# Channel-attention plus channel-mix kernel: covariance rows of batch 1 moved into block 0's up projection, warm-up matmuls after the first x projection, squares in pairs, and a last block that computes its gates first

## Chip, cores, metric

One NeuronCore of one Trainium2 chip. The metric is device microseconds of one execution. All runs told of here count as fast ones. A run repeats only to a few microseconds (the kernel before took 530.3 to 534.9 us in the three calls below), so the text relies on ratios within one call (kernels that ran on the same chip, round by round) and, for where the time goes, on distances inside the profiles.

PE is TensorE, PEld its weight loads, DVE VectorE, ACT ScalarE, POOL GpSimd, SP the queue of SyncE.

## The reference, cut to what matters

Inputs q, k, v are (4, 6208, 256) in float32.

```python
qn = q / (norm(q, axis=1) + 1e-6);  kn = k / (norm(k, axis=1) + 1e-6)
a  = softmax(kn^T @ qn / tau)              # 256 x 256 for each of 4 batches
x  = v @ a                                 # 6208 x 256 for each batch
xk = mu_k * x + (1 - mu_k) * x_prev;  xr = mu_r * x + (1 - mu_r) * x_prev   # x_prev: the row before
out = sigmoid(xr @ w_r) * (relu(xk @ w_k) ** 2 @ w_v)                       # d_ff = 1024
```

A batch has 12 blocks of 512 rows and 64 rows over. The kernel runs 48 full blocks and one last block of 4 x 64 = 256 rows that gathers what is over ("left").

## The kernel before

Batch 0's covariance (k^T q and the sums of squares) comes first, alone. Then a loop over blocks, cut in eight steps j, interleaves on PE: the up projection of block i+1, the down projection of block i, the x projection (v times attention) of block i+2, and one *unit* (one row tile of the covariance of the next batch) in some of the steps. Per group of four units PE also adds up the squares (`group_norms`), and after batch 1's 49 units a chain of 16 small pieces makes its softmax.

```python
def unit_square(b, g, s):                      # ACT: squares of one row tile, 128 x 512
    rows, _ = rows_of(b, g)
    qk, qk2 = groups[b, g][:2]
    nc.scalar.activation(qk2[:rows, s], qk[:rows, s], AF.Square)

def up(i, fh):                                 # PE, then ACT
    ...
    nc.scalar.activation(kr[:, :m], kT_ps[:, :m], AF.Relu, scale=0.5 ** 0.5)

def down(i, j):                                # PE: a gate and 8 matmuls for each 128 rows
    ...
def finish(i, s):
    nc.scalar.activation(res[:, s], vr_ps[:, D:], AF.Tanh, scale=0.5)
    nc.vector.scalar_tensor_tensor(res[:, s], res[:, s], 1.0, vr_ps[:, :D], op0=OP.add, op1=OP.mult)
    if (s + 1) * P == size(i):
        if i < NBLK - 1:
            ...                                # one store of the block
        else:
            for b in range(B):                 # last block: four stores, one queue
                s, o = divmod(b * L, P)
                nc.sync.dma_start(out[b, NB * M:, :], res[o:o + L, s, :])
...
# order of the loads: w_k, group 0, v(1), group 1, w_r, w_v, v(2), group 2, then in the loop v(3), ...
halves()                                       # batch 0's softmax
x_first()                                      # x projection of block 0
v_transpose_pe(1, nc.scalar.copy)()            # needs v of block 1
early = units[:S + 1]                          # group 0 (1 row tile) and group 1 (4) of batch 1
for u in early:
    unit_matmul(*u, late=True)                 # needs k of group 1
for u in early[:3]:
    unit_square(*u)
keep_warm(4)                                   # matmuls that only keep PE busy
for i in range(-2, NBLK):
    for j in range(8):
        ...
        up(i + 1, j)
        ...
        if i == -1 and j == 6:
            v_transpose_pe(2, nc.vector.tensor_copy)()     # needs v of block 2
        if i == -1 and j == 7:
            group_norms(1, 0); group_norms(1, 1)
        slots = () if i < 0 else (1, 2, 3, 4, 5, 7) if i < 8 else (1, 3, 4, 5, 7)
        if j in slots and ...: unit()
```

Of the kernel before, what the change touches and what calls it, by code (L numbers as in the profile page):

```python
# [10 lines left out]
F32 = mybir.dt.float32  # L11
BF16 = mybir.dt.bfloat16
AX = mybir.AxisListType.X
AF = mybir.ActivationFunctionType
OP = mybir.AluOpType
# [3 lines left out]
def kernel(  # L19
# [13 lines left out]
    nc = tc.nc  # L33
    B, N, C = q.shape
# [48 lines left out]

    cov = {}
    groups = {}
    DIRECT = NB - 3

    def sizes(b):
        return [1] + [S] * (NB - 1) + ([S // 2] * 2 if b == 0 else [S])
# [5 lines left out]
    def rows_of(b, g):  # L95
        return (P if g else L), sizes(b)[g]
# [29 lines left out]
            nc.scalar.activation(qk2[:rows, :n, i, :], t_f[i][:rows, :n], AF.Square)  # L126

    def unit_square(b, g, s):
        rows, _ = rows_of(b, g)
        qk, qk2 = groups[b, g][:2]  # L130
        nc.scalar.activation(qk2[:rows, s], qk[:rows, s], AF.Square)

    def unit_matmul(b, g, s, late=False):
        rows, n = rows_of(b, g)
        t0 = g == order(b)[0] and s == 0
        te = g == len(sizes(b)) - 1 and s == n - 1
        if t0:

            cov[b] = (ps.tile([P, 2, C], F32, name="s_ps", tag="s_ps" if b else "vr_ps", bufs=1 if b else 2),
                      ps.tile([P, 2 * C], F32, name="ssq_ps", tag="ssq_ps" if b else "vr_ps", bufs=1 if b else 2))  # L140
        s_ps = cov[b][0] if b or g <= DIRECT else cov["s"]
        qk = groups[b, g][0]
        for ih in range(2):
            nc.tensor.matmul(s_ps[:, ih, :], qk[:rows, s, 1, ih * P:(ih + 1) * P],  # L144
                             qk[:rows, s, 0, :], start=t0 and ih == 0, stop=te,
                             skip_group_check=True)
        if s == n - 1 and not late:
            if b == 0 and g > DIRECT:
                norms_direct(g)
            else:  # L150
                group_norms(b, g)

    def group_norms(b, g):

        rows, n = rows_of(b, g)
        ssq_ps = cov[b][1]
        qk2 = groups[b, g][1]
        for u in range(n):
            nc.tensor.matmul(ssq_ps[32 * u:32 * (u + 1)], ones[:rows, :32],  # L159
                             qk2[:rows, u].rearrange("p i c -> p (i c)"),  # L160
                             start=g == (1 if u or b == 0 else 0), stop=g == (len(sizes(b)) - 1 if b else DIRECT), tile_position=(0, 32 * u),
                             skip_group_check=True)

    def norms_direct(g):

# [106 lines left out]
    def size(i):  # L272
        return M if i < NBLK - 1 else B * L
# [14 lines left out]
    def v_transpose_pe(i, evac):  # L288

        v_bf = st.pop((i, "v"))  # L290
        vT_ps = ps.tile([P, S, 2, P], BF16, name="vT_ps", tag="kT_ps", bufs=3)
        for s in range(S):
            for h in range(2):
                nc.tensor.transpose(vT_ps[:, s, h], v_bf[:, s, h * P:(h + 1) * P], ident)

        def go():
            vT = p2.tile([P, S, 2, P], BF16, name="vT", tag="vT", bufs=4)
            evac(vT, vT_ps)
            st[i, "vT"] = vT
        return go  # L300
# [18 lines left out]
    def x_first():  # L319

        xT = p2.tile([P, 2, M + 1], BF16, name="xT", tag="xT", bufs=3)
        st[0, "x"] = xT
        nc.vector.memset(xT[:, :, 0:1], 0.0)
        vT = st[0, "vT"]
        x_ps = [ps.tile([P, M], F32, name="xT_ps", tag="vr_ps", bufs=2) for dh in range(2)]
        for ih in range(2):
            for dh in range(2):
                nc.tensor.matmul(x_ps[dh], a_sb[:, 0, ih, dh * P:(dh + 1) * P], vT[:, :, ih, :],
                                 start=ih == 0, stop=ih == 1)
        nc.scalar.copy(xT[:, 0, 1:], x_ps[0])  # L330
        nc.vector.tensor_copy(xT[:, 1, 1:], x_ps[1])
# [66 lines left out]
    def down(i, j):  # L398

        s, h = divmod(j, 2)  # L400
        if s * P >= size(i):
            return
        kk = st[i, "kk"]
        if j == 0:
            st[i, "res"] = p2.tile([P, S, D], F32, name="res", tag="res", bufs=3)
        if h == 0:
            vr_ps = ps.tile([P, 2 * D], F32, name="vr_ps", tag="vr_ps", bufs=2)
            st[i, "vr"] = vr_ps
            xr = st[i, "xr"]
            for dh in range(2):  # L410
                nc.tensor.matmul(vr_ps[:, D:], xr[:, dh, s * P:(s + 1) * P], w_r_sb[:, dh, :],  # L411
                                 start=dh == 0, stop=dh == 1)
        vr_ps = st[i, "vr"]
        for fh in (range(3) if h == 0 else range(3, 8)):
            nc.tensor.matmul(vr_ps[:, :D], kk[:, fh, s * P:(s + 1) * P], w_v_sb[:, fh, :],  # L415
                             start=fh == 0, stop=fh == 7)

    def finish(i, s):
        if s * P >= size(i):
            return  # L420
        res = st[i, "res"]
        vr_ps = st[i, "vr"]

        nc.scalar.activation(res[:, s], vr_ps[:, D:], AF.Tanh, scale=0.5)  # L424
        nc.vector.scalar_tensor_tensor(res[:, s], res[:, s], 1.0, vr_ps[:, :D], op0=OP.add, op1=OP.mult)  # L425
        if (s + 1) * P == size(i):
            if i < NBLK - 1:
                b, t = blocks[i]
                nc.sync.dma_start(out[b, t * M:(t + 1) * M, :].rearrange("(s p) c -> p s c", p=P), res)
            else:  # L430
                for b in range(B):
                    s, o = divmod(b * L, P)
                    nc.sync.dma_start(out[b, NB * M:, :], res[o:o + L, s, :])



# [84 lines left out]
    keep_warm(7)  # L521
    halves()
    x_first()
    v_transpose_pe(1, nc.scalar.copy)()

    early = units[:S + 1]
    pos["mm"] = pos["sq"] = S + 1
    for u in early:
        unit_matmul(*u, late=True)
    for u in early[:3]:  # L530
        unit_square(*u)
    keep_warm(4)


    left_go = {}
    left = {}
    for i in range(-2, NBLK):
        for j in range(8):
            if j % 2 == 0:
                if j == 0 and i >= 1:  # L540
                    finish(i - 1, 3)
                elif j > 0 and i >= 0:
                    finish(i, j // 2 - 1)
            if j == 0 and 3 <= i + 5 < NBLK - 1:
                v_load(i + 5)
            if chain:
                piece = chain.pop(0)
                if piece is not None:
                    piece()
            if 0 <= i + 1 < NBLK:  # L550
                up(i + 1, j)
            if i >= 0:
                if j == 0 :
                    square(i, 7)
            if j > 0 and 0 <= i + 1 < NBLK:
                square(i + 1, j - 1)
            if i >= 0:
                down(i, j)
            if i + 2 < NBLK:
                n = i + 2  # L560
                full = 0 < n < NBLK - 1
                if j == 0 and full:
                    x_half(n, 0)
                if j == 2 and full:
                    x_half(n, 1)
                if j == 3:
                    mix_delta(n)
                if j in (4, 5):
                    mix(n, "xk", j - 4)
                if j == 7:  # L570
                    mix(n, "xr", 0)
            if j == 1 and 0 <= i + 1 < NBLK:
                mix(i + 1, "xr", 1)
            if i == -1 and j == 6:
                v_transpose_pe(2, nc.vector.tensor_copy)()
            if j == 5 and 3 <= i + 4 < NBLK - 1:
                v_transpose(i + 4)
            b = (i + 2) // NB
            if i == -1 and j in (3, 5):
                unit_square(*early[3 if j == 3 else 4])  # L580
            if i == -1 and j == 7:
                group_norms(1, 0)
                group_norms(1, 1)
            if i < 0:
                slots = ()
            elif i < 8:
                slots = (1, 2, 3, 4, 5, 7)
            else:
                slots = (1, 3, 4, 5, 7)
            if j in slots and pos["mm"] < len(units) and units[pos["mm"]][0] <= b + 1:  # L590
                unit()
            if i >= 0 and i % NB == 2 and j == 1 and i // NB < B:
                left_go[0] = left_x(i // NB)
            if i >= 0 and i % NB == 4 and j == 4 and i // NB < B:
                left_go[0][0]()
            if i >= 0 and i % NB == 6 and j == 4 and i // NB < B:
                left_go[0][1]()


# [33 lines left out]
```

## Time and profile before

534.54 us, median of 3 runs (534.12 to 535.59).

| what | value | view |
|---|---|---|
| profiled span | 532.8 us | page |
| PE, ACT busy | 95%, 82% | page |
| PE waiting, 60 to 526 us | 1.0 us in all | table of waits |
| first x projection, block 0's down stage | 41.82, 58.37 us | timeline |
| last block: first gate, last multiply's end, end of span | 525.19, 528.73, 532.8 us | timeline |

Lines of the page: the span, busy us of PE and ACT, and the clock granted to PE in 40 slices, in tenths.

```profile
span 532.8 us, 10152 instructions
...
PE 507.3 (95%) x3590; PEld 336.5 (63%) x3651; DVE 408.6 (77%) x962; ACT 434.4 (82%) x883; POOL 102.2 (19%) x143
...
PEclk9997999999999999999999999999999999999999
```

The table of waits of PE from 60 to 526 us (us in total, times, longest):

```profile
PE kT_ps L386 <- DVE xk L371: 1.0, 2, 0.5
```

The steady part has nothing to win for PE. The ends have. The clock, in windows of 3 us (length, then busy us of PE, PEld, DVE, ACT, POOL; then the granted clock, DMA share, GB/s):

```profile
42.00:45.00 3.00, 1.20 (x9) 0.40 (x8) 2.17 (x5) 0.59 (x1) 1.81 (x3) 1.00 1.42 195
45.00:48.00 3.00, 1.22 (x12) 0.70 (x9) 1.64 (x4) 2.06 (x3) 1.99 (x4) 0.59 1.46 198
48.00:51.00 3.00, 3.00 (x12) 1.51 (x10) 0.00 (x0) 0.63 (x2) 1.44 (x3) 0.50 1.46 195
51.00:54.00 3.00, 2.95 (x12) 1.16 (x11) 1.31 (x3) 1.93 (x4) 1.76 (x3) 0.77 1.45 197
```

The timeline of PE alone, around the start of block 0 (start, us, engine, line, operation, tiles, count, and in brackets the idle time before it and what ended it):

```profile
41.82 1.10 PE L328 MATMUL xT_ps<-vT,a_sb 128*128 128x512 bf16 x4 [0.29 <-DVE a_sb L256]
44.72 0.62 PE L294 MATMUL vT_ps<-ident,v_bf 128*128 128x128 bf16 x8 [1.80 <-DMA v_bf<-in_v_dram]
...
47.44 1.89 PE L144 MATMUL s_ps<-qk 128*128 128x256 bf16 x8 [1.78 <-DMA qk<-in_k_dram]
49.12 1.91 PE L444 MATMUL junk_ps<-fill,ones 128*128 128x512 bf16 x4
50.83 1.06 PE L386 MATMUL kT_ps<-xk,w_k_sb 128*128 128x512 bf16 x2
...
57.28 0.39 PE L159 MATMUL ssq_ps<-qk_464,ones 64*32 64x512 bf16 x1
...
57.93 0.60 PE L386 MATMUL kT_ps<-xk,w_k_sb 128*128 128x512 bf16 x2
58.37 0.38 PE L411 MATMUL vr_ps<-w_r_sb,xr 128*128 128x256 bf16 x2
```

Line 328 is block 0's x projection. PE then waits 1.80 us for v of block 1 and 1.78 us for k of group 1, and the clock falls to half: the eight covariance matmuls at 47.44 and the four warm-up matmuls at 49.12 take 0.43 us for each 512 columns and not 0.22. Line 386 is the up projection, line 411 a gate of the down stage.

The end, all engines:

```profile
525.19 0.38 PE L411 MATMUL vr_ps<-w_r_sb,xr 128*128 128x256 bf16 x2
...
525.40 1.36 PE L415 MATMUL vr_ps<-w_v_sb,kk 128*128 128x256 bf16 x8
...
526.48 0.10 PEld L415 LDWEIGHTS <-kk 128*128 128x128 bf16 x1 [0.43 <-DVE kk L396]
...
527.67 2.46 SPq L433 DMA_DIRECT2D out_dram<-res  x4
527.89 0.38 ACT L424 ACTIVATE res<-vr_ps 128x256 f32<-128x256 f32 x1 [0.71 <-PE vr_ps L415]
528.31 0.42 DVE L425 SCALAR_TENSOR_TENSOR res<-res,vr_ps 128x256 f32<-128x256 f32 x1 [0.67 <-ACT res L424]
```

The gate at 525.19 and its 8 matmuls, of which the eighth waits for a square until 526.48, then the second half; its tanh (527.89), its multiply (528.31), and four stores that one queue issues one after the other.

### The profile page before, as it was taken

Reading aid. Unit: us, or ns where it says so; the run is one execution under the profiler, and the core shown is the slowest. Engines: PE = TensorE matmul, PEld = TensorE weight load, DVE = VectorE, ACT = ScalarE, POOL = GpSimd, SP = SyncE. Lnnn points to the kernel's source line nnn. Section 1 sums busy time; section 2 is a strip of 40 time slices with the busy share of each in tenths; the row PEclk is TensorE's granted clock in tenths of the full one; section 3 lists DMA queues with packets and bytes.
Section 4 is the critical chain, followed back from the end, with each engine's and each line's share of the span. In section 5 each row is a group of like instructions: output and inputs, shape, how many; then the busy total and the mean of one; then the engine's idle time right before and its main releaser. Section 6 shows DMA issues by size and latency. Waiting matters only on the chain.

```text
span 532.8 us, 10152 instructions
## 1 busy us (share of the span) xinstructions
PE 507.3 (95%) x3590; PEld 336.5 (63%) x3651; DVE 408.6 (77%) x962; ACT 434.4 (82%) x883; POOL 102.2 (19%) x143
## 2 busy tenths in 40 slices
PE   4977999999999999999999999999999999999996
PEld 1453566666666666666666666666666666666675
DVE  4554787777898777777798777877898989888883
ACT  6884999898788888888778888888878777777773
POOL 0055423221311231322041322310030101000000
PEclk9997999999999999999999999999999999999999
DMA  8999999999599999999498999995286565433212
GB/s 302 421 283 185 190 191 199 197 168 132 76 208 157 166 196 156 157 168 163 84 189 152 133 198 175 137 189 115 61 138 139 103 139 112 110 86 94 80 41 98
DMA packets 143722, 83.76 MB, mean 157 GB/s; under 512 B 51700, under 2 KB 140088, under 8 KB 143672
## 3 DMA queue, kind: packets, MB, share of 16 engines
q0 software_dynamic: 65808, 33.01, 51.5%
q1 hardware_dynamic: 77856, 50.11, 37.9%
q8 instruction: 28, 0.46, 0.3%
q14 instruction: 22, 0.18, 0.1%
q10 hardware_dynamic: 8, 0.00, 0.0%
HBM read 78.71 MB, written 25.43 MB: 195 GB/s over the span
## 4 chain that ended last, share of the span: by engine, by line
PE 86%; DMA 7%; DVE 3%; ACT 1%; issue 1%; POOL 1%; SPq 0%; ACTq 0%
PE vr_ps L415 32%; PE kT_ps L386 29%; PE vr_ps L411 8%; PE xT_ps L315 7%; PE s_ps L144 6%; PE ssq_ps L159 2%; DMA f_339<-in_k_dram 2%; DMA f_235<-in_k_dram 2%; DMA qk<-in_k_dram 2%; DMA f_130<-in_k_dram 1%; DVE xk L371 1%; ACT kr L390 1%; DVE kk L396 1%; DVE res L425 0%; PE bank L194 0%
## 5 line engine op out<-in xcount | busy, mean ns | idle before, releaser
L390 ACT ACTIVATE kr<-kT_ps 128x512 bf16<-128x512 f32 (+1 forms) x392 | 232.9, 596 | 48.7 <-PE kT_ps L386 28.6
L415 PE MATMUL vr_ps<-w_v_sb,kk 128*128 128x256 bf16 x1552 | 233.1, 273 | 2.0
L386 PE MATMUL kT_ps<-xk,w_k_sb 128*128 128x512 bf16 (+1 forms) x726 | 219.9, 378 | 1.5 <-DVE xk L371 1.0
L415 PEld LDWEIGHTS <-kk 128*128 128x128 bf16 x1552 | 151.9, 98 | 58.7 <-DVE xT L308 0.6
L396 DVE TENSOR_TENSOR kk<-kr 128x512 bf16<-128x512 bf16 (+1 forms) x392 | 155.0, 415 | 7.7 <-ACT kr L390 7.1
L425 DVE SCALAR_TENSOR_TENSOR res<-res,vr_ps 128x256 f32<-128x256 f32 x194 | 81.2, 419 | 76.9 <-ACT res L424 74.9
L386 PEld LDWEIGHTS <-w_k_sb 128*128 128x128 bf16 x784 | 73.6, 98 | 36.8 <-issue 9.3
L144 PE MATMUL s_ps<-qk 128*128 128x256 bf16 (+1 forms) x392 | 73.2, 288 | 7.1 <-DVE qk L124 5.3
L317 ACT CAST xT<-xT_ps 128x512 bf16<-128x512 f32 x94 | 55.3, 588 | 29.3 <-PE xT_ps L315 29.1
L424 ACT ACTIVATE res<-vr_ps 128x256 f32<-128x256 f32 x194 | 74.0, 381 | 2.3 <-PE vr_ps L415 1.7
L411 PE MATMUL vr_ps<-w_r_sb,xr 128*128 128x256 bf16 x388 | 74.1, 273 | 0.7
L371 DVE SCALAR_TENSOR_TENSOR xk<-delta,mu_t,xT 128x512 bf16<-128x512 bf16 x96 | 71.4, 744 | 0.0
L371 DVE SCALAR_TENSOR_TENSOR xr<-delta,mu_t,xT 128x512 bf16<-128x512 bf16 x96 | 71.4, 744 | 0.0
L411 PEld LDWEIGHTS <-xr 128*128 128x128 bf16 x388 | 37.9, 98 | 46.0 <-issue 2.0
L118 POOL DMA_DIRECT2D qk<-in_q_dram x39 | 29.0, 742 | 181.4 <-ACT res L424 32.3
L315 PE MATMUL xT_ps<-vT,a_sb 128*128 128x512 bf16 x188 | 56.3, 381 | 0.0
L144 PEld LDWEIGHTS <-qk 128*128 128x128 bf16 (+1 forms) x392 | 38.7, 102 | 19.3 <-DVE qk L124 8.2
L278 POOL DMA_DIRECT2D v_bf<-in_v_dram x48 | 37.2, 776 | 66.6 <-DMA vT<-v_bf 62.2
L361 DVE TENSOR_TENSOR delta<-xT 128x1024 bf16<-128x1024 bf16 x48 | 33.2, 692 | 14.1 <-ACT xT L317 14.0
L118 POOL DMA_DIRECT2D qk<-in_k_dram x39 | 29.0, 743 | 2.6 <-DMA w_v_sb<-in_moe_w_v_dram 1.6
L315 PEld LDWEIGHTS <-a_sb 128*128 128x128 bf16 x188 | 18.5, 98 | 2.9 <-issue 0.6
L206 POOL TENSOR_TENSOR rn<-rn,half 128x4 f32<-128x4 f32 x3 | 3.2, 1073 | 63.1 <-DVE rn L203 63.1
(218 smaller groups left out, 242.8 us busy)
## 6 DMA issues: line engine op xcount, KB each, us to landing
out_dram<-res SPq DMA_DIRECT2D x48, 512.0 KB, 3.5
v_bf<-in_v_dram POOLq DMA_DIRECT2D x48, 256.0 KB, 7.9
qk<-in_q_dram POOLq DMA_DIRECT2D x36, 256.0 KB, 5.9
qk<-in_k_dram POOLq DMA_DIRECT2D x36, 256.0 KB, 8.0
vT<-v_bf SPq DMA_TRANSPOSE x45, 5.5
f_104<-in_q_dram SPq DMA_DIRECT2D x1, 512.0 KB, 3.8
f_106<-in_k_dram SPq DMA_DIRECT2D x1, 512.0 KB, 5.0
f_128<-in_q_dram SPq DMA_DIRECT2D x1, 512.0 KB, 5.8
```

The costliest lines, as they stand in the source:

```text
L118: nc.gpsimd.dma_start(qk[:rows, :n, i, :], qk_src(t, b, g))
L144: nc.tensor.matmul(s_ps[:, ih, :], qk[:rows, s, 1, ih * P:(ih + 1) * P], qk[:rows, s, 0, :], start=t0 and ih == 0, stop=te, skip_group_che ...
L315: nc.tensor.matmul(xT_ps, a_sb[:, b, ih, dh * P:(dh + 1) * P], vT[:, :, ih, :], start=ih == 0, stop=ih == 1)
L317: nc.scalar.copy(xT[:, dh, 1:], xT_ps)
L371: nc.vector.scalar_tensor_tensor(o[:, dh], st[i, "d"][:, dh], mu[:, dh:dh + 1], st[i, "x"][:, dh, :M], op0=OP.mult, op1=OP.add)
L386: nc.tensor.matmul(kT_ps[:, :m], w_k_sb[:, dh, fh * P:(fh + 1) * P], xk[:, dh, :m], start=dh == 0, stop=dh == 1)
L390: nc.scalar.activation(kr[:, :m], kT_ps[:, :m], AF.Relu, scale=0.5 ** 0.5)
L396: nc.vector.tensor_tensor(st[i, "kk"][:, fh, :m], kr[:, :m], kr[:, :m], op=OP.mult)
L411: nc.tensor.matmul(vr_ps[:, D:], xr[:, dh, s * P:(s + 1) * P], w_r_sb[:, dh, :], start=dh == 0, stop=dh == 1)
L415: nc.tensor.matmul(vr_ps[:, :D], kk[:, fh, s * P:(s + 1) * P], w_v_sb[:, fh, :], start=fh == 0, stop=fh == 7)
L424: nc.scalar.activation(res[:, s], vr_ps[:, D:], AF.Tanh, scale=0.5)
L425: nc.vector.scalar_tensor_tensor(res[:, s], res[:, s], 1.0, vr_ps[:, :D], op0=OP.add, op1=OP.mult)
```

## The change

Its intent: start block 0's up projection without waiting for covariance data, and put the first covariance rows of batch 1 into it where PE waits for ACT; keep PE busy with nine warm-up matmuls after the first x projection, so that the clock does not fall; spare ACT some fixed cost by squaring two row tiles at once; and shorten the last block's serial end.

```diff
     def unit_square(b, g, s):
-        nc.scalar.activation(qk2[:rows, s], qk[:rows, s], AF.Square)
+        if s % 2 == 0:
+            e = min(s + 2, n)
+            nc.scalar.activation(qk2[:rows, s:e], qk[:rows, s:e], AF.Square)
...
+    def last_block(i):
+        ...                                   # gates of both halves first
+        square(i, 7)
+        finish(i - 1, 3)
+        for s in range(SL):
+            nc.scalar.activation(res[:, s], r_ps[:, s], AF.Tanh, scale=0.5)
+        for s in range(SL):
+            for fh in range(8):
+                nc.tensor.matmul(y_ps[s], kk[:, fh, s * P:(s + 1) * P], w_v_sb[:, fh, :], ...)
+            nc.vector.scalar_tensor_tensor(res[:, s], res[:, s], 1.0, y_ps[s], op0=OP.add, op1=OP.mult)
+            for h in range(P // L):
+                (nc.sync, nc.scalar)[h % 2].dma_start(out[s * P // L + h, NB * M:, :], res[h * L:(h + 1) * L, s])
...
     x_first()
+    keep_warm(7)
     v_transpose_pe(1, nc.scalar.copy)()
+    keep_warm(2)
-    for u in early:
-        unit_matmul(*u, late=True)
-    for u in early[:3]:
-        unit_square(*u)
-    keep_warm(4)
...
-                if j == 7:
+                if j == 7 and n != 1:
                     mix(n, "xr", 0)
+            if i == 0 and j == 6:
+                mix(1, "xr", 0)
...
-            if i == -1 and j in (3, 5):
-                unit_square(*early[3 if j == 3 else 4])
+            if i == -1 and j in (5, 6):
+                for u in early[:2] if j == 5 else early[2:]:
+                    unit_matmul(*u, late=True)
+            if (i, j) in ((0, 1), (0, 5), (1, 3)):
+                unit_square(*early[{(0, 1): 0, (0, 5): 1, (1, 3): 3}[i, j]])
-            if i == -1 and j == 7:
+            if i == 0 and j == 7:
                 group_norms(1, 0)
+            if i == 2 and j == 0:
                 group_norms(1, 1)
+            elif i == 0:
+                slots = (3, 5, 7)
+            elif i == 1:
+                slots = (1, 2, 4, 5, 7)
```

Cut: `start=` of the norms now follows from which rows were summed already, block 47 is stored in two halves, and the loop ends one block earlier, with `last_block` called behind it.

More of the change, by code (lines that the diff above doesn't have):

```diff
@@ L85 @@
     groups = {}
+    summed = set()
     DIRECT = NB - 3
@@ L128, in unit_square @@
     def unit_square(b, g, s):
-        rows, _ = rows_of(b, g)
+        rows, n = rows_of(b, g)
         qk, qk2 = groups[b, g][:2]
-        nc.scalar.activation(qk2[:rows, s], qk[:rows, s], AF.Square)
+        if s % 2 == 0:
+            e = min(s + 2, n)
+            nc.scalar.activation(qk2[:rows, s:e], qk[:rows, s:e], AF.Square)
     def unit_matmul(b, g, s, late=False):
@@ L160, in group_norms @@
                              qk2[:rows, u].rearrange("p i c -> p (i c)"),
-                             start=g == (1 if u or b == 0 else 0), stop=g == (len(sizes(b)) - 1 if b else DIRECT), tile_position=(0, 32 * u),
+                             start=(b, u) not in summed, stop=g == (len(sizes(b)) - 1 if b else DIRECT), tile_position=(0, 32 * u),
                              skip_group_check=True)
+            summed.add((b, u))
     def norms_direct(g):
@@ L400, in down @@
         s, h = divmod(j, 2)
-        if s * P >= size(i):
+        if s * P >= size(i) or i == NBLK - 1:
             return
@@ L418, in finish @@
     def finish(i, s):
-        if s * P >= size(i):
+        if i == NBLK - 1:
             return
@@ L425, in finish @@
         nc.vector.scalar_tensor_tensor(res[:, s], res[:, s], 1.0, vr_ps[:, :D], op0=OP.add, op1=OP.mult)
-        if (s + 1) * P == size(i):
-            if i < NBLK - 1:
-                b, t = blocks[i]
-                nc.sync.dma_start(out[b, t * M:(t + 1) * M, :].rearrange("(s p) c -> p s c", p=P), res)
-            else:
-                for b in range(B):
-                    s, o = divmod(b * L, P)
-                    nc.sync.dma_start(out[b, NB * M:, :], res[o:o + L, s, :])
+        b, t = blocks[i]
+        dst = out[b, t * M:(t + 1) * M, :].rearrange("(s p) c -> p s c", p=P)
+        if i < NBLK - 2:
+            if s == S - 1:
+                nc.sync.dma_start(dst, res)
+        elif s % 2:
+            nc.sync.dma_start(dst[:, s - 1:s + 1], res[:, s - 1:s + 1])
+    def last_block(i):
+        kk, xr = st[i, "kk"], st[i, "xr"]
+        SL = B * L // P
+        res = p2.tile([P, S, D], F32, name="res", tag="res", bufs=3)
+        r_ps = ps.tile([P, SL, D], F32, name="r_ps", tag="s_ps")
+        y_ps = [ps.tile([P, D], F32, name="y_ps", tag=tag) for tag in ("ssq_ps", "xT_ps")[:SL]]
+        for s in range(SL):
+            for dh in range(2):
+                nc.tensor.matmul(r_ps[:, s], xr[:, dh, s * P:(s + 1) * P], w_r_sb[:, dh, :],
+                                 start=dh == 0, stop=dh == 1)
+        square(i, 7)
+        finish(i - 1, 3)
+        for s in range(SL):
+            nc.scalar.activation(res[:, s], r_ps[:, s], AF.Tanh, scale=0.5)
+        for s in range(SL):
+            for fh in range(8):
+                nc.tensor.matmul(y_ps[s], kk[:, fh, s * P:(s + 1) * P], w_v_sb[:, fh, :],
+                                 start=fh == 0, stop=fh == 7)
+            nc.vector.scalar_tensor_tensor(res[:, s], res[:, s], 1.0, y_ps[s], op0=OP.add, op1=OP.mult)
+            for h in range(P // L):
+                (nc.sync, nc.scalar)[h % 2].dma_start(out[s * P // L + h, NB * M:, :], res[h * L:(h + 1) * L, s])
     nc.scalar.dma_start(mu_rows[0:2], moe_mu_k.rearrange("(h p) -> h p", p=P))
@@ L523 @@
     x_first()
+    keep_warm(7)
     v_transpose_pe(1, nc.scalar.copy)()
+    keep_warm(2)
     early = units[:S + 1]
     pos["mm"] = pos["sq"] = S + 1
-    for u in early:
-        unit_matmul(*u, late=True)
-    for u in early[:3]:
-        unit_square(*u)
-    keep_warm(4)
     left_go = {}
     left = {}
-    for i in range(-2, NBLK):
+    for i in range(-2, NBLK - 1):
         for j in range(8):
@@ L597 @@
                 left_go[0][1]()
+    last_block(NBLK - 1)
 _INS = ['q', 'k', 'v', 'tau', 'moe_mu_k', 'moe_mu_r', 'moe_w_k', 'moe_w_v', 'moe_w_r']
```

## The prediction

> **What bounds the kernel now.** The page gives PE 95% busy, ACT 82%, DVE 77% of a 532.8 us span. The table of waits finds only 1.0 us of PE waiting between 60 and 526 us: no PE work is taken from there. What is open is the two ends.
>
> Head (windows and timeline, 40 to 58 us): after the first x projection PE idles 42.9 to 44.7 (waits for block 1's v) and 45.7 to 47.4 (waits for k of batch 1's group 1). The granted clock falls to 0.50 from about 45.6 to 52.4, two periods of 3.4 us, which is the window length that the Trainium skill gives ("TensorE: Matmul & The Clock Gate", Part 1). So 512 columns take 0.43 us instead of 0.22 there. Block 0's up projection starts at 50.83, although its input xk was ready at 45.9; block 0's down stage starts with the up matmuls at 57.93.
>
> Tail (timeline from 524 us): the last block waits about 0.4 us for square 7, then gate, 8 matmuls, tanh (0.38), multiply (0.42), and four stores in a row on one queue, 0.55 us of issue each, from 527.7 to 529.5; end 532.8.
>
> **What the change does.**
> 1. Warm-up matmuls fill the first gap, block 0's up starts as soon as xk is there (about 46), and the early covariance work goes into it. That phase is then paced by ACT (about 0.49 us per relu or copy when packed, timeline) and by v of block 2, which lands only at about 52.5. The transposes of that v sit before the last up piece, so PE stands 50.4 to 52.6. I estimate block 0's down stage at about 54.3 instead of 57.9: 3.6 us. 0.65 us of norm matmuls only move later, so 3.0 remain. The new hole may drop the clock once more (PE about 40% busy in that window): 0 to 1.7 us lost. The transposed v of block 3 lands at about 65.4 (issue 56.05 + 9.3) and is wanted at about 64.8: 0 to 0.6 lost. Net for the head 2.2 us.
> 2. Squares in pairs: one of 1024 takes 1.06 us (the same square in the prologue), two of 512 take 0.63 each alone but 0.52 packed. About 0.1 us per pair, 8 us of ACT time in all, but PE waits for ACT hardly anywhere: 0 to 0.5 us of span.
> 3. Batch 1's units are postponed (3 and 5 in blocks 0 and 1, not 6): they end at the end of block 7, so the softmax chain ends just before its weights are wanted: 0 to 0.5 us lost.
> 4. Tail: gates first hide the wait for square 7 (0.45), tanh leaves the end (0.4), the last store is issued at about 527.9 rather than 529.5. Gain 1.9 us.
>
> **Time.** 534.5 - 2.2 - 1.9 = about 530.4 us; 8 in 10: 528.6 to 532.6. Faster by over 2% (under 523.9) 0.02, within 2% 0.97, slower 0.01.
>
> **What would show it.** Clock 1.0 from 46 to 50; first relu of block 0 at about 46.5, not 51.9; a PE wait of about 2 us for v of block 2; a possible clock dip near 52 to 56; block 1's first x projection at about 64.8, not 69.3; ACT busy about 426 us; the last stores issued at 527.9 less the head's gain.
>
> **What would make it wrong.** A clock that stays up in the hole (1 us better); a transfer that lands later because loads are asked for sooner (worse); ACT falling behind in block 0, where squares crowd; a PE stall at block 12's x projection for the softmax weights.

## The result

531.34 us, median of 4 runs (530.82 to 532.13), against 534.46 us (534.12 to 535.59) for the kernel before; ratio 0.9939, 95% interval 0.9919 to 0.9959. A ratio is the mean time of one kernel's fast runs over that of the other's of the same rounds, so not quite the ratio of the medians that are quoted. The prediction was 530.4 us with a range of 528.6 to 532.6: inside the range, with a gain of 4.1 us foretold and 3.1 measured. The gain is under 1%.

The lines of the page that answer to those of before:

```profile
span 529.2 us, 10156 instructions
...
PE 508.7 (96%) x3656; PEld 335.3 (63%) x3656; DVE 405.9 (77%) x962; ACT 425.8 (80%) x811; POOL 102.2 (19%) x143
...
PEclk9999999999999999999999999999999999999999
```

```profile
PE kT_ps L391 <- DVE xk L376: 1.0, 2, 0.5
PE vr_ps L416 <- DVE xr L376: 0.6, 1, 0.6
```

PE's waits in the steady part are no fewer: one for an xr mix has come. (ACT has 8.6 us less to do over the whole span.) The windows of the start:

```profile
42.00:45.00 3.00, 2.32 (x13) 0.96 (x13) 2.17 (x5) 0.59 (x1) 2.14 (x3) 1.00 1.40 188
45.00:48.00 3.00, 2.76 (x19) 1.37 (x18) 2.33 (x5) 2.32 (x4) 1.59 (x3) 1.00 1.45 198
48.00:51.00 3.00, 2.82 (x15) 1.00 (x12) 2.70 (x7) 2.87 (x7) 1.48 (x2) 1.00 1.46 196
51.00:54.00 3.00, 1.81 (x18) 1.39 (x19) 2.32 (x5) 0.52 (x2) 1.66 (x3) 1.00 1.45 198
```

The clock holds in this profile. The timeline of PE (line 333 is the first x projection, 472 warm-up, 391 up, 148 covariance, 416 a gate):

```profile
41.55 1.10 PE L333 MATMUL xT_ps<-vT,a_sb 128*128 128x512 bf16 x4 [0.29 <-DVE a_sb L261]
42.49 1.67 PE L472 MATMUL junk_ps<-fill,ones 128*128 128x512 bf16 x7
44.84 0.62 PE L299 MATMUL vT_ps<-ident,v_bf 128*128 128x128 bf16 x8 [0.68 <-DMA v_bf<-in_v_dram]
...
45.73 0.59 PE L391 MATMUL kT_ps<-xk,w_k_sb 128*128 128x512 bf16 x2
...
49.68 0.71 PE L148 MATMUL s_ps<-qk 64*128 64x256 bf16 x4
...
52.19 0.62 PE L299 MATMUL vT_ps<-ident,v_bf 128*128 128x128 bf16 x8 [1.37 <-DMA v_bf<-in_v_dram]
...
54.16 0.38 PE L416 MATMUL vr_ps<-w_r_sb,xr 128*128 128x256 bf16 x2
...
64.81 0.39 PE L416 MATMUL vr_ps<-w_r_sb,xr 128*128 128x256 bf16 x2 [0.57 <-DVE xr L376]
```

The up projection starts at 45.73 and not at 50.83. PE then stands 1.37 us for v of block 2, as foretold, and block 0's down stage begins at 54.16 and not at 58.37. In the last line is a wait that was not foretold: block 1's first gate waits 0.57 us for the xr mix that the change had moved.

The end:

```profile
522.83 0.60 PE L449 MATMUL r_ps<-w_r_sb,xr 128*128 128x256 bf16 x4
...
523.27 1.91 PE L457 MATMUL y_ps<-w_v_sb,kk 128*128 128x256 bf16 x16
...
523.47 0.66 ACT L454 ACTIVATE res<-r_ps 128x256 f32<-128x256 f32 x2
...
524.85 1.37 SPq L461 DMA_DIRECT2D out_dram<-res  x2
524.85 1.45 ACTq L461 DMA_DIRECT2D out_dram<-res  x2
525.29 0.42 DVE L459 SCALAR_TENSOR_TENSOR res<-res,y_ps 128x256 f32<-128x256 f32 x1 [0.47 <-PE y_ps L457]
```

Four gate matmuls hide the wait for the square, both tanh are done at 524.13, and the stores go out on two queues.

### Where 3.6 us of span came from

Four distances split each profile. They repeat far better than the total. "Lead-in" is from the first x projection to block 0's first gate; "body" from the x projection of block 2 to that of block 12; "rest" from there to block 47's; "end" from there to the end of the span. (Between lead-in and body lie 0.55 us in every run.)

| profile | first x projection at | lead-in | body | rest | end | span |
|---|---|---|---|---|---|---|
| before | 41.82 | 16.55 | 102.60 | 342.01 | 29.27 | 532.8 |
| changed | 41.55 | 12.61 | 104.61 | 341.85 | 28.03 | 529.2 |
| difference | -0.27 | -3.94 | +2.01 | -0.16 | -1.24 | -3.6 |

So the head won 3.9 us and gave 2.0 of them back in the next ten blocks; the end won 1.2 us. In these two profiles the loads land alike (v of block 1 at 44.67 and 44.80 us, v of block 2 at 52.06 and 52.14), so this difference is not one of load times. The experiments ask what each of these is due to.

### The profile page after: what moved, and what is told of

The parts are those of the page before. It is cut to its first block, busy times and chain, and to the rows that moved or that the text cites. A ratio compares the mean times of both kernels' runs of the same rounds, so it can differ in the third digit from the quotient of the medians.

```text
span 529.2 us, 10156 instructions
## 1 busy us (share of the span) xinstructions
PE 508.7 (96%) x3656; PEld 335.3 (63%) x3656; DVE 405.9 (77%) x962; ACT 425.8 (80%) x811; POOL 102.2 (19%) x143
## 4 chain that ended last, share of the span: by engine, by line
PE 87%; DMA 7%; DVE 2%; POOL 1%; issue 1%; ACT 0%; SPq 0%; ACTq 0%; DVEq 0%; POOLq 0%
PE kT_ps L391 31%; PE vr_ps L420 31%; PE vr_ps L416 8%; PE xT_ps L320 7%; PE s_ps L148 6%; PE ssq_ps L163 2%; DMA f_339<-in_k_dram 2%; DMA f_235<-in_k_dram 2%; DMA v_bf<-in_v_dram 2%; DMA f_130<-in_k_dram 1%; DVE xk L376 1%; POOL qk L119 1%; PE bank L199 0%; DVE kk L401 0%; POOL v_bf L283 0%
## 5 line engine op out<-in xcount | busy, mean ns | idle before, releaser
L391 PE MATMUL kT_ps<-xk,w_k_sb 128*128 128x512 bf16 (+1 forms) x784 | 231.5, 377 | 1.0 <-DVE xk L376 1.0
L420 PEld LDWEIGHTS <-kk 128*128 128x128 bf16 x1536 | 150.3, 98 | 58.7 <-DVE xT L313 0.6
L148 PE MATMUL s_ps<-qk 128*128 128x256 bf16 (+1 forms) x392 | 71.6, 282 | 6.4 <-DVE qk L125 6.4
L283 POOL DMA_DIRECT2D v_bf<-in_v_dram x48 | 37.2, 776 | 71.9 <-DMA vT<-v_bf 62.5
```

Of the source, the lines that this page charges most:

```text
L148: nc.tensor.matmul(s_ps[:, ih, :], qk[:rows, s, 1, ih * P:(ih + 1) * P], qk[:rows, s, 0, :], start=t0 and ih == 0, stop=te, skip_group_che ...
L391: nc.tensor.matmul(kT_ps[:, :m], w_k_sb[:, dh, fh * P:(fh + 1) * P], xk[:, dh, :m], start=dh == 0, stop=dh == 1)
L420: nc.tensor.matmul(vr_ps[:, :D], kk[:, fh, s * P:(s + 1) * P], w_v_sb[:, fh, :], start=fh == 0, stop=fh == 7)
```

## The experiments

My theory: the two ends add up; the lead-in was long through the clock, and the order of work and the warm-up matmuls share the gain; the body grew by 0.65 us of norms that only moved and by new waits. Rivals: the warm-ups alone, or the order alone, made the lead-in short. Twelve runs (eleven kernels, the changed one twice) came in three calls of four, each with 5 rounds beside the kernel before, all with right results.

| call and run | median us | ratio to before, 95% interval | first x projection | lead-in | body | rest | end |
|---|---|---|---|---|---|---|---|
| 1 e1_tail_only | 530.36 | 0.9973 (0.9952 to 0.9994) | 44.80 | 11.18 | 102.62 | 342.02 | 28.04 |
| 1 e2_head_only | 531.07 | 0.9988 (0.9968 to 1.0007) | 41.26 | 10.73 | 105.11 | 341.85 | 29.30 |
| 1 e4_no_warm | 531.84 | 0.9999 (0.9979 to 1.0019) | 43.37 | 12.08 | 105.02 | 341.85 | 28.03 |
| 1 e5_warm_only | 531.36 | 0.9994 (0.9975 to 1.0013) | 41.25 | 13.09 | 102.60 | 342.50 | 29.31 |
| 2 e0_after_again | 530.55 | 0.9970 (0.9942 to 0.9998) | 41.96 | 10.44 | 105.01 | 341.84 | 28.01 |
| 2 e6_one_queue | 531.89 | 0.9986 (0.9959 to 1.0014) | 42.06 | 11.72 | 105.01 | 341.84 | 28.72 |
| 2 e9_v23_xr | 529.97 | 0.9958 (0.9933 to 0.9983) | 41.57 | 10.43 | 105.28 | 342.10 | 27.97 |
| 2 e12_warm_tail | 529.39 | 0.9952 (0.9926 to 0.9978) | 41.36 | 13.00 | 102.60 | 342.01 | 27.98 |
| 3 e17_after_third | 530.72 | 0.9970 (0.9944 to 0.9996) | 43.58 | 10.46 | 105.02 | 341.85 | 28.05 |
| 3 e16_catch_up | 529.71 | 0.9955 (0.9924 to 0.9985) | 42.04 | 10.45 | 104.36 | 342.07 | 28.03 |
| 3 e13_warm_tail_no4 | 529.85 | 0.9955 (0.9928 to 0.9982) | 42.29 | 11.94 | 102.60 | 342.00 | 28.02 |
| 3 e15_plus_pairs | 529.67 | 0.9953 (0.9926 to 0.9981) | 43.97 | 12.27 | 102.60 | 342.05 | 28.06 |

The kernel before took 532.37, 532.10 and 532.29 us (medians of 11) in the three calls, 2 us less than in its own first runs, and from 530.3 to 534.9 us from run to run. Between profiles of the same code it is the start that differs: in the changed kernel's three the span is 529.2, 527.8 and 529.5 us and block 0's first gate comes at 54.16, 52.40 and 54.04 us, while body, rest and end repeat within 0.1 us for the same code, but for 0.4 us in one body (changed kernel, first profile) and 0.5 us in one rest (e5_warm_only).

Two things move the start. In eight of these twelve profiles, e0_after_again and e17_after_third among them, the clock was at half speed for 3.4 to 10.2 us between 30 and 41 us, before the first x projection. And v of block 2 landed between 50.0 and 52.7 us (at 48.5 in e9_v23_xr, which loads it earlier): with the changed head the lead-in is 10.4 to 10.7 us in the five profiles with the warm-ups in which PE does not wait for it, and 12.61 and 11.72 us in the two in which it does (1.37 us in the first profile, 1.06 in e6_one_queue).

### e1_tail_only: the end alone

```diff
 (kernel before)
+ last_block(), called after the loop; finish() and down() as in the change
-    for i in range(-2, NBLK):
+    for i in range(-2, NBLK - 1):
```

> The kernel before with the new end alone (gates first, two queues). Theory 1, the two ends add up: the profiled span ends 1.2 us earlier than before counted from the first gate matmul of the last block (6.4 us instead of 7.6), about 533.2 us in all, ratio 0.998. Rival: part of the tail's gain only exists behind the new head, then under 0.6 us (534.0). Block 1 and later x projections stay where they were before (69.3, 101.5 us).

The end took 28.04 us and not 29.27: 1.23 us won, with the old head and the old body. Ratio 0.9973, about 1.4 us. So the end is worth 1.2 us in the profile by itself. A miss: the x projections were not where they were before (66.95 and 99.13 us, not 69.3 and 101.5), because this run's start differed: its clock had fallen at 30 us, its first x projection came 3 us later, the loads had landed by then, and PE hardly waited (0.5 us for k) in a lead-in of 11.18 us. The old head can thus have a short lead-in by chance; still, its first gate came at 55.98 us, 2.4 earlier than in the kernel before's profile, although the loads landed alike (v of block 1 at 44.70 us).

### e2_head_only: the head alone

```diff
 (changed kernel)
- last_block() and its call; finish() and down() as before
```

> The changed kernel with the old end. Theory 1: the lead over the kernel before, read at the x projection of block 30, stays 2.36 us; total about 532.2 us, ratio 0.9957. Rival, the ends are not independent: lead or tail differ from this by more than 0.5 us.

The end is the old one (29.30 us), so the two do add up in the profile. In time the head alone won 0.6 us here with an interval that holds 0; not the 2.3 us expected. The lead over the kernel before can't be read across chips whose starts differ, so that part of the expectation could not be tested as I had put it.

### e4_no_warm: the new order without the warm-up matmuls

```diff
 (changed kernel)
     x_first()
-    keep_warm(7)
     v_transpose_pe(1, nc.scalar.copy)()
-    keep_warm(2)
```

> The changed kernel without the 7 and 2 warm-up matmuls after the first x projection; order of work as changed. Theory A, clock and order share the head's gain: the clock drops to half at about 45.6 us, up matmuls of block 0 take 0.43 us, block 0's down stage starts at 55 instead of 54.2, total 1.0 to 1.5 us more than the changed kernel (532.5). Rival B, the warm-ups are the whole head gain: total 533.6 or more. Rival C, the order alone: total within 0.4 us of the changed kernel, because ACT paces the phase and v of block 2 lands at 52.2 anyway.

The clock fell, though v of block 1 was not waited for here; PE waited 1.8 us for the first xk mix instead:

```profile
45.00:48.00 3.00, 0.89 (x4) 0.30 (x3) 2.86 (x5) 1.11 (x2) 1.88 (x4) 0.96 1.45 196
48.00:51.00 3.00, 3.00 (x8) 1.03 (x7) 1.98 (x5) 2.23 (x4) 1.60 (x3) 0.50 1.46 197
```

Lead-in 12.08 us, 1.4 to 1.6 more than in the five profiles with the warm-ups and no wait for v of block 2. In the same call the end alone (e1_tail_only) took 530.43 us on average and this kernel, which has the same end, 531.79: without the warm-ups the moved rows cost 1.4 us. e2_head_only, the same head with the warm-ups, took 531.10 us in this call with the old end; less 1.2 us for the end that is 529.9, so the warm-ups are worth about 1.9 us with the new order (1.1 to 2.7 by the scatter of the runs), where theory A has 1.0 to 1.5. Rival C (the order alone) falls. The expected dip came at 47.7 and not 45.6 us.

### e5_warm_only: the warm-up matmuls in the old order

```diff
 (kernel before)
     x_first()
+    keep_warm(7)
     v_transpose_pe(1, nc.scalar.copy)()
+    keep_warm(2)
```

> The kernel before with the 7 and 2 warm-up matmuls added after its first x projection, order of work as before. The covariance matmuls still wait for k until 47.4. Theory A: clock stays at 1.0, block 0's up starts at about 49.3 instead of 50.8, its down stage at about 55 instead of 58.4, lead at block 30 of 1.5 to 2.8 us, total about 532. Rival B (warm-ups are all of it): lead 2.4 or more. Rival C (order alone): lead under 0.7.

The clock stayed at 1.0; the up projection started at 47.5 and the down stage at 54.34 us, both before theory A's 49.3 and 55. But k had landed at 45.8 and not at 47.4 us, so this is not the warm-ups' doing alone (more under e12_warm_tail). In time the gain over the kernel before is 0.3 us and not resolved (0.9975 to 1.0013), nor is the difference from e2_head_only (0.9988). One other part of the rest was 0.5 us longer than in the kernel before; it lies in blocks 32 and 33, 0.24 us in each, while the softmax chain of the last batch runs. I did not find out why, and e12_warm_tail, with the same loop, does not have it.

### e0_after_again and e17_after_third: the changed kernel beside the others

> The changed kernel once more, beside the other runs of this call, because the kernel before was 2 us faster on the chip of the first call than in its own runs. Theory, the end is worth 1.2 us everywhere and the head's worth depends on when the loads land and whether the clock drops: ratio 0.993 to 0.998. Rival, a fixed gain of 3.1 us: ratio 0.993 to 0.995. In the profile, from block 2's x projection to block 12's it takes 2.0 us (or more) longer than in the kernel before (102.6 us), of which 0.65 are the postponed norms.

> The changed kernel once more, as the yardstick of this call. Theory: body from block 2's to block 12's x projection 104.6 to 105.1 us again, and ratio to the kernel before between 0.993 and 0.998.

Both gave 0.997, about 1.6 us, of which the end is 1.2. The fixed gain of 3.1 us (0.994) lies just outside both intervals, which begin at 0.9942 and 0.9944. What is left for the head on these chips is about 0.4 us, and that is known only to about 1.5 us either way. Body 105.0 us both times, 2.4 more than in the kernel before. Where it is lost, in windows between x projections, first the kernel before (its block 0, then its block 9), then the changed kernel (same):

```profile
58.92:69.34 10.42, 10.37 (x77) 7.06 (x76) 7.63 (x19) 10.04 (x23) 3.70 (x5) 1.00 1.55 185
...
152.84:161.52 8.68, 8.63 (x62) 5.86 (x60) 8.39 (x23) 7.46 (x18) 0.00 (x0) 1.00 1.39 212
```

```profile
52.94:63.60 10.66, 10.04 (x69) 6.38 (x68) 7.64 (x19) 10.29 (x20) 2.22 (x3) 1.00 1.40 190
...
148.22:157.95 9.73, 9.50 (x63) 6.09 (x62) 9.66 (x27) 7.82 (x19) 0.00 (x0) 1.00 1.32 196
```

Block 0 has three units and some norms less to do: from 10.42 us take 3 x 0.22 (units) and 0.44 (the norms of a group: block 1 has one group more than block 0 and takes 10.87 us, not 10.43), add 0.32 (the norms of group 0, 57.28 to 57.60 in the timeline of before), and about 9.65 us should do. It takes 10.66, with ACT busy 97% of it. That is 1.0 us lost; 0.57 of it stands as the wait for xr. Block 9 takes 9.73 and not 8.68 us, of which 0.43 are one piece of the softmax chain that now falls into it: 0.6 us lost, with DVE 99% busy. The rest of the 2.4 us are the norms of groups 0 and 1, which left the lead-in (0.75 us by the same durations).

### e6_one_queue: the last four stores on one queue

```diff
-  (nc.sync, nc.scalar)[h % 2].dma_start(...)
+  nc.sync.dma_start(...)
```

> The changed kernel with the last four stores on one queue. Theory: from the end of the last multiply to the end of the span it takes 0.5 us longer than in the changed kernel (4.0 us instead of 3.5). Rival, the queues do not matter since the landing of the last store sets the end: within 0.15 us.

```profile
524.86 2.46 SPq L461 DMA_DIRECT2D out_dram<-res  x4
```

The end takes 28.72 us and not 28.01: the second queue is worth 0.7 us (0.5 expected), and gates first with the early tanh the other 0.5. From the last multiply's end to the end of the span it is 4.19 us (changed kernel of this call: 3.47; kernel before: 4.07). The rest of this profile's loss lies in its start (a wait of 1.1 us for v of block 2) and has nothing to do with the edit. The Trainium skill says that issuing from several engines only saves the sequencer's issue time ("Trainium Kernel Development and Optimization", Key Constraints); that agrees: four issues of about 0.55 us stand in one row here, in two rows of two there, and the 0.7 us saved is less than the two issues that left the row.

### e9_v23_xr: the two named waits taken away

```diff
-    nc.gpsimd.dma_start(w_v_sb, ...)
     v_load(2)
-    next_load()                       # group 2
+    nc.gpsimd.dma_start(w_v_sb, ...)
...
                 v_load(i + 5)
+                if i == -2:
+                    next_load()       # group 2, now behind v of block 3
...
-                if j == 7 and n != 1:
+                if j == 7:
                     mix(n, "xr", 0)
-            if i == 0 and j == 6:
-                mix(1, "xr", 0)
```

> The changed kernel with v of block 2 loaded ahead of w_v, v of block 3 ahead of batch 1's group 2, and block 1's first xr mix put back to where it was. Theory, the hole before v of block 2's transposes and the late xr mix cost the changed kernel up to 1.4 us and 0.57 us: both waits vanish from the table of PE waits; total 0.6 to 1.6 us less than the changed kernel of this call. Rival, the waits were slack (ACT paces the phase, and w_v or group 2 now land too late): within 0.4 us or slower.

The waits for v and for xr are gone, and block 0 takes 9.91 us and not 10.66. But block 1 takes 11.66 and not 10.64, with a new wait:

```profile
63.32 0.60 PE L420 MATMUL vr_ps<-w_v_sb,kk 128*128 128x256 bf16 x4
64.76 0.28 PE L420 MATMUL vr_ps<-w_v_sb,kk 128*128 128x256 bf16 x1 [0.84 <-DVE kk L401]
```

PE waits for a square on DVE, that for a relu on ACT, and ACT stood 0.6 us ahead of its third pair of squares, at 62.59; k of that group, issued at 48.80, has a time to landing of 13.7 us, which puts it at 62.5. (The profile names PE as the releaser; that it was this load is read from the times, and no run takes it apart.) The body is 105.28 us: the 0.57 us wait was slack, as the rival has it. The total is 0.6 us under the changed kernel's of this call by medians and 0.5 by means, inside the spread. The lead-in was the same 10.43 us in both, because v of block 2 landed in time in both; whether the earlier load helps where it lands late was not seen.

### e16_catch_up: batch 1's units finished as early as before

```diff
+            elif i < 6:
+                slots = (1, 2, 3, 4, 5, 6, 7)
             elif i < 8:
                 slots = (1, 2, 3, 4, 5, 7)
```

> The changed kernel with seven instead of six units in blocks 2 to 5, so that batch 1's units and its softmax chain end where they do in the kernel before (in block 7). Theory, the later chain costs 0.2 to 0.6 us in block 9 (vector engine behind, the matmuls after the spread wait): block 11's to block 12's x projection takes 8.7 us again instead of 9.3 to 9.7, and the body from block 2 to block 12 shrinks by 0.2 to 0.8 us. Rival, the loss moves into the crowded blocks 2 to 5: body unchanged within 0.15 us or longer.

```profile
148.71:157.40 8.69, 8.69 (x63) 5.86 (x61) 8.18 (x23) 7.47 (x19) 0.00 (x0) 1.00 1.42 205
```

Block 9 is back at 8.69 us and the body shrinks to 104.36, by 0.66 us: theory. So the late softmax chain costs the changed kernel this much. The rest is 0.22 us longer (342.07, not 341.85), all of it in block 33, as in e9_v23_xr; whether the edit has a part in that is not known. In time: 529.71 against 530.72 us in the same call.

### e12_warm_tail: all but the moved rows and pairs

```diff
 (kernel before, with the edits of e1_tail_only and e5_warm_only)
```

> The kernel before with the warm-up matmuls and the new end, but neither the moved covariance rows nor the paired squares nor the postponed units. Theory, what the move of the rows wins before block 0 it gives back in blocks 0 to 10: total within 0.5 us of the changed kernel of this call. Rival, the move carries the head's gain: 1.0 us or more slower than the changed kernel.

529.39 us against 530.55 for the changed kernel in the same call. Its lead-in is 13.00 us, 2.6 longer, and its body 102.60 us, 2.4 shorter: what the moved rows win before block 0 they give back by block 12. It was expected within 0.5 us of the changed kernel and took 0.8 less on average. So my theory that order and warm-ups share the gain holds for the lead-in only; for the total, that the warm-ups are what is left of the head (rival B) fits better. The clock holds without the moved rows:

```profile
45.00:48.00 3.00, 2.61 (x17) 1.53 (x18) 1.46 (x4) 2.30 (x4) 1.48 (x2) 1.00 1.45 198
48.00:51.00 3.00, 3.00 (x15) 1.32 (x14) 2.11 (x5) 2.83 (x6) 0.84 (x2) 1.00 1.46 197
```

What the half clock cost in the old order can be read from the first covariance matmul of group 1 to block 0's first gate, which leaves the load times out:

```profile
45.78 1.05 PE L144 MATMUL s_ps<-qk 128*128 128x256 bf16 x8 [0.34 <-DMA qk<-in_k_dram]
...
54.36 0.38 PE L411 MATMUL vr_ps<-w_r_sb,xr 128*128 128x256 bf16 x2
```

It takes 8.58 us here, 8.58 in e1_tail_only and 8.57 in e5_warm_only, all at full clock, but 10.93 in the kernel before (47.44 to 58.37). So the half clock cost 2.4 us there, and of the 4.2 us by which the changed kernel's first gate came earlier about 1.9 are left for the order of work.

The warm-ups in the old order were never seen with late loads: in e5_warm_only and here v of block 1 and k of group 1 landed 1.7 to 2.7 us earlier than in the kernel before. An estimate: without the new warm-ups PE would have been busy for 47% and 40% of the clock's window that holds them, and after every window under half the clock was low (see the last section).

### e13_warm_tail_no4 and e15_plus_pairs

```diff
 (e12_warm_tail)
     for u in early[:3]:
         unit_square(*u)
-    keep_warm(4)
```

> The kernel before with the warm-up matmuls, the new end, and without its old 4 warm-up matmuls after the covariance rows (they stand between these rows and block 0's up projection for 0.9 us). Theory: block 0's down stage starts 0.9 us earlier than in the run with them (12.1 us after the first x projection instead of 13.0), body still 102.6 us, total 0.7 to 1.2 us under the changed kernel's plus what that run already had; ratio to the kernel before 0.991 to 0.995. Rival, ACT paces the phase from its squares on, so that nothing is won: 13.0 again.

```diff
 (e13_warm_tail_no4)
+ unit_square() as in the change: two row tiles at once
```

> The run before this one with the squares of two rows in one instruction. Theory: ACT has 0.1 us less to do per pair but relu waits up to 1.06 us behind one: span within 0.5 us of the run without, ACT busy 7 us less. Rival 1, ACT was in the way in blocks 0 to 7: 0.5 us or more faster. Rival 2, the longer instruction holds relu and tanh up: 0.5 us or more slower, body over 103 us.

Without the 4 old warm-ups the lead-in is 11.94 us, 1.1 shorter, and the body stays 102.60. With pairs the body is again 102.60 us and the rest 342.05 against 342.00: squares in pairs take 8.6 us of ACT's time away (433.9 to 425.3 us) and nothing of the body's or the rest's. (The lead-in is 0.33 us longer: PE waits 0.83 us for a relu in it and not 0.41.) Medians 529.85 and 529.67 us, and 530.72 for the changed kernel in this call.

These versions (e12, e13, e15, e16) are the fastest that ran. On average they took 0.8 to 0.9 us less than the changed kernel of their call, four times in the same direction, but each ratio lies inside the other's interval. They beat the kernel before clearly, by 2.3 to 2.6 us on average; that they beat the changed kernel is likely and not shown.

## Why the prediction was right, and where it was wrong

- **Total.** Right within its range (530.4 foretold, 531.34 measured). The gain was over-estimated by 1.0 us, and in the later calls it was 1.6 us, not 4.1. There luck had a part: the same sum, taken from the 532.2 us that the kernel before took in those calls, would have given 528.1 us, below the range; the changed kernel took 530.55 and 530.72.
- **Tail, the step that failed in size.** "Gain 1.9 us" was 1.24 (the term of the stores, 1.05 by what the other two leave of 1.9, was 0.58), and the end repeats: 27.97 to 28.06 us in ten profiles with the new one on two queues, 29.27 to 29.31 in three with the old. By its parts, counted from the first gate: the last matmul ended 0.32 us earlier (2.35 against 2.67; foretold 0.45), tanh took 0.34 us off what lies between the last matmul and the last multiply's end (0.53 against 0.87; foretold 0.4), and from there to the end of the span 3.49 us were needed and not 4.07: 0.58. I had read the gain of the stores from the moment the last one is issued (527.9 instead of 529.5). That moment did come 1.4 us earlier (2.9 us after the first gate, not 4.3), but 0.66 of this was the earlier multiply, which I had already counted, and the last store's way to the end did not shorten.
- **Head, start.** Right in its mechanism for the profiled pair: up at 45.73 (about 46 foretold), relu at 46.41 (46.5), a wait for v of block 2 (1.37 us of PE idle, 2 foretold), down stage 4.2 us earlier (3.6). The clock stayed up in that hole, so the 0 to 1.7 us set aside for it were not needed, nor the 0 to 0.6 for the transposed v of block 3.
- **Head, what is given back.** The 0.65 us of norms was about right (0.75). "ACT falling behind in block 0, where squares crowd" stood only under what could go wrong; block 0 lost 1.0 us with ACT busy 97%. How much of this is ACT's is not shown: 0.57 us stands as the wait for xr, and with that wait gone (e9_v23_xr) block 0 took 0.75 us less but block 1 1.0 us more. The softmax chain cost 0.2 us in the first profile (block 9: 9.33 us, where 8.68 + 0.43 = 9.11 would do) and 0.6 in the others (foretold 0 to 0.5), and e16_catch_up shows that it came from the later units and chain. It was not the named stall at block 12's x projection, which never appears in the waits; DVE was full in block 9.
- **Squares.** Right: about 8 us of ACT time, nothing of the span that shows (e15_plus_pairs). The Trainium skill gives 186 ns + 0.833 ns per element for such an instruction, when its scale and bias are immediate values, and an overlap of about 93 ns between two in a row ("ScalarE: Activation LUTs", What ACT_TABLE_LOAD costs). From this I estimate 1.04 us for 1024 elements, 0.61 for 512, 0.09 won per pair; the traces have 1.05 and 0.63, and 0.12 per pair (8.6 us over 72 pairs).
- **What I had not seen.** I took the kernel before's dip of the clock for a fixed part of it. It changes from run to run: of the two profiles of the old head it stands in one (kernel before) and not in the other (e1_tail_only). In the later calls the head is worth about 0.4 us (1.6 us by ratio 0.997, less 1.2 for the end), not 2; that the dip was missing there is likely, but the kernel before was not profiled in those calls. And the moved rows, which I took for the core of the head's gain, carry none of it that lasts beyond block 12: without them, with the warm-ups, the kernel was no slower (e12_warm_tail).

What stays open: how much of the 2 us between the first runs and the later calls is the dip. The mean clock of the kernel before's runs does not say: in call 2 its runs with a mean clock of 0.992 or less took 533.5 us on average and those with 0.996 or more 531.3 us; in call 1 531.9 and 532.0; in call 3 532.9 and 532.1. As I read the two profiles of the old head, a dip at 30 us, while loads still bind, delays the first x projection and is partly made up after it; one at 45 us is not; the mean does not tell them apart. That the warm-ups pay in time, and not only in the traces, e4_no_warm against e2_head_only shows for the new order; for the old order e5_warm_only (0.3 us) did not resolve it.

## What to carry to other kernels

Work moved out of a hole has to go somewhere: before moving it, add up each engine's time in the stage that receives it (here ACT was at 96% in block 0 already), and measure from a point behind that stage, not at the hole. When two waits end close together, taking the one that the profile names away may only show the next. At the end of a kernel, count from the last result to the last byte, and count each microsecond once; gates first, an early tanh and a second queue were worth 1.2 us together, the safest part of this change.

## What the Trainium skill lacked or had wrong

- "TensorE: Matmul & The Clock Gate", Part 1, has the clock fall after an idle window of about 3.4 us and advises against gaps over 3.4 us. The length agrees (half clock from 45.55 to 52.38 us, two windows of 3.41 us). But no gap was that long: in the window before the drop, 42.14 to 45.55 us, PE was busy 1.61 us and the longest gap was 1.80 us. In each of the 14 profiles the changes of the clock lie a whole number of 3.413 us apart, so that the windows can be laid over the trace. Between the first full clock and the last block, the clock was at half speed after all nine windows in which PE was busy for less than half (38 to 49%), with no gap over 2.0 us. Of the fuller windows at full clock only two were followed by a drop (76% in e0_after_again, 73% in e16_catch_up). The changed kernel's hole lies in a window with 60% (2.04 us busy of 50.00 to 53.41), and the clock stayed up. PE's busy time is modelled, so these shares are rough. The page tells of one kernel whose clock fell through short idle times between bursts, but gives no such share.
- "DMA: Bandwidth & Descriptors", Anatomy of one DMA — SWDGE (gpsimd) path, gives about 2.0 us plus bytes over 436 GB/s for one DMA; from this I estimate 2.6 us for the 256 KB of a v or k load. In the kernel before, with several such loads queued behind one another, it took 8.9 us (v of block 2) to 14.7 us (k of a later group) from issue to landing. That section has no figure for loads that queue.
- No page has the time from a program's last packet to its own last instruction: 1.6 us, with the old end and with the new one (last packet's end at 531.23 of 532.8, and 527.62 of 529.2 us). About 0.3 us of it pass until the last store's semaphore is full, the other 1.2 in semaphore waits and drains at the program's last line.
